# The second pair's second chunk takes its running sum from the whole first chunk instead of a carried row

## The chip, the cores and the metric

One core of a Trainium2 chip runs the whole program. The metric is the device time of one execution in microseconds (us). The core's engines are named as the profile names them: PE does matrix products, DVE is the vector engine, ACT the scalar engine, POOL the GpSimd engine, and SP only issues transfers. PEld is PE's weight load, which overlaps its products.

## What is computed

A linear attention with a complex decay feeds two layers of experts. Cut to what matters:

```python
mag = np.sqrt(a_re * a_re + a_im * a_im)
scale = np.minimum(mag, 0.999) / (mag + 1e-06)
a_re_n, a_im_n = (a_re * scale, a_im * scale)
for t in range(S):                       # S = 768, for 2 batches and 8 heads of 48
    S_re, S_im = (ar * S_re - ai * S_im + kv, ar * S_im + ai * S_re)
    y[:, :, t] = np.einsum('bhd,bhde->bhe', q[:, :, t], S_re)
h = x @ w_in                             # x: 1536 tokens x 384, w_in: 384 x 2048
x = (np.maximum(h, 0.0) + np.log1p(np.exp(-np.abs(h)))) @ w_out
for e in range(4):                       # four experts of 384 x 1024 x 384
    out += p[:, e:e + 1] * (np.maximum(x @ w1[e], 0.0) @ w2[e])
```

## The kernel before

**Attention in chunks.** The 1536 tokens are twelve chunks of 128, six to a batch. They are handled in six pairs `n` = 0 to 5, chunks `c` = 0 and 1 of each. The product of decays from the batch's start to a token is a running sum of logarithms: a phase (the angle, in `im`) and a magnitude (in `t`). `prefix(n, c, what)` makes the running sum inside a chunk by one product with a triangle of ones (`trik` for phases, `tri` for magnitudes) into a PSUM tile `pf` or `pl`. `wrap` takes whole turns out of the phase (ACT at L590, then DVE at L591), `level` copies the magnitude out (ACT, L597). `carry` takes the last row of both (ACT at L607 for the phase), and two small transfers on SP's queue (L608, L609) put them into the tile `rows`. The next chunk's `prefix` adds that row to its own first row with POOL (L564), so that the triangle product carries on from it.

Pair 0 does without a row: its second chunk's product starts with the whole first chunk times a matrix of ones (`onek` or `ones`, L582), and the triangle product adds to that. Pairs 3 to 5 split their operands in two (L570 on) and use a carried row too.

**Around it.** `squares`, `ratio` and `logmag` prepare angle and magnitude (POOL adds the two squares at L537 for every pair but the first). `trig` makes cosine and sine on ACT. Sine and arc tangent need another table of functions than exponential and logarithm, so both sit in an `excursion` between two table loads (L97). `s3_units` is the attention of one chunk: `prep` multiplies queries and keys by decay and angle (DVE, L643 and two of L655 into `QK`), `turn` transposes them on PE (L664, tile `tp`; ACT copies them out at L665), `score` makes the score products (`sp`, L673) that DVE masks into `A` (L674), `mix` makes the output `yps` (L689), `state` the running state `S` (`sps`, L700; DVE L704, L706), and `done` writes the output in two parts into `X`, the high one on ACT (L711), the low one on DVE (L712).

**Weights.** The first layer's weights come in as wide numbers. DVE joins them in three steps (L70, L71, L72 into `f`), ACT casts the high part (L181) and DVE subtracts for the low part (L182). Four pairs of such tiles (A and B) are needed for each block of the first layer, whose products are at L232 (into `h`) and L319 (into `y`). Every product of the first block, tokens 0 to 255, waits for `X` of pair 0.

**What sets the order.** The program is written as units, each put at a place on a time line (`put`), and the framework's scheduler then lays the instructions of each engine out in one order at build time. An engine runs its instructions strictly in that order. The three PSUM buffers of the tag `a` are handed out in turn to `pf`, `pl`, `sp`, `sps` and others. The change touches `prefix` and `s2_units`; the line that places the units of pair 1 stays, and spreads them from -8 to 0 on the time line:

```python
put([lambda: logmag(1, both)] + s2_units(1) + [lambda: s1_load(2), lambda: squares(2, both), lambda: ratio(2, both)]
    + [excursion(lambda: trig(1), lambda: arctan(2))], -8, 0)
```

## Time and profile before

| | |
|---|---|
| time, median of 3 runs | 737.78 us (737.22 to 738.26) |
| time of the profiled execution | 738.36 us |
| its span, first to last instruction | 736.6 us |
| PE busy | 702.5 us (95%) |
| DVE busy | 586.4 us (80%) |
| ACT busy | 487.4 us (66%) |
| POOL busy | 32.3 us (4%) |
| mean granted clock of PE | 0.988 |

The time is 1.8 us more than the span: that is what lies around the instructions. The span is read from the engine that is busy nearly all of it, PE, and a stretch is of interest where PE is not.

### The profile page before, as it was taken

How to read it: one execution, taken by the hardware profiler on the slowest of the kernel's cores; microseconds unless marked ns; L12 is line 12 of the kernel's file. 1: busy time of each engine (PE TensorE's matmuls, PEld its weight loads, DVE VectorE, ACT ScalarE, POOL GpSimd, SP SyncE). 2: the span in 40 equal slices, each digit the busy share in tenths (PEclk: the TensorE clock that was granted, in tenths of full speed). 3: DMA queues.
4: the chain of work that ended last, by engine and by line, in shares of the span. 5: the costliest groups of instructions: out<-in, count | busy, mean ns of one | idle time of the engine just before them, and what ended most of it. 6: DMA issues, size and time to landing. Idle time of an engine off the chain costs nothing.

```text
span 736.6 us, 13285 instructions
## 1 busy us (share of the span) xinstructions
PE 702.5 (95%) x5159; PEld 674.9 (92%) x5159; DVE 586.4 (80%) x1149; ACT 487.4 (66%) x898; POOL 32.3 (4%) x31
## 2 busy tenths in 40 slices
PE   2789999999999999999999999999999999999996
PEld 1468899999899999999999999999999999999996
DVE  6999999955875854548888779988778898998963
ACT  7887976888896856345686665555556567766640
POOL 1122010000111001000000000000000000000000
PEclk9699999999999999999999999999999999999998
DMA  7665666621211420121022120213445345455401
GB/s 268 195 191 179 201 203 192 224 77 44 86 45 59 122 80 2 59 86 44 23 86 65 43 87 21 87 44 109 119 157 155 127 151 172 150 172 152 162 31 69
DMA packets 36342, 83.56 MB, mean 113 GB/s; under 512 B 4528, under 2 KB 13232, under 8 KB 36272
## 3 DMA queue, kind: packets, MB, share of 16 engines
q1 hardware_dynamic: 36272, 82.64, 35.5%
q8 instruction: 42, 0.69, 0.4%
q14 instruction: 28, 0.23, 0.1%
HBM read 73.95 MB, written 8.65 MB: 112 GB/s over the span
## 4 chain that ended last, share of the span: by engine, by line


## 5 line engine op out<-in xcount | busy, mean ns | idle before, releaser
L232 PE MATMUL h<-X,A 128*128 128x384 f32 (+1 forms) x936 | 175.9, 329 | 2.3 <-ACT A L181 0.8
L232 PEld LDWEIGHTS h<-X,A 128*128 128x128 f32 x936 | 153.4, 188 | 5.6 <-issue 1.6
L319 PE MATMUL y<-B,g 128*128 128x384 f32 x744 | 150.2, 335 | 0.2 <-DVE acc L350 0.2
L319 PEld LDWEIGHTS y<-B,g 128*128 128x128 f32 x744 | 131.0, 188 | 0.7 <-issue 0.5
L319 PE MATMUL y<-g,B 128*128 128x384 f32 (+1 forms) x504 | 91.0, 315 | 0.3 <-ACT g L285 0.3
L319 PE MATMUL z<-B,g 128*128 128x384 f32 x372 | 84.7, 334 | 0.0
L319 PEld LDWEIGHTS y<-g,B 128*128 128x128 f32 x504 | 79.3, 189 | 2.0 <-ACT g L285 0.6
L319 PEld LDWEIGHTS z<-B,g 128*128 128x128 f32 x372 | 66.3, 188 | 0.0
L247 ACT ACTIVATE e<-h 128x384 f32<-128x384 f32 (+1 forms) x60 | 30.8, 512 | 37.1 <-PE h L232 36.0
L250 DVE SCALAR_TENSOR_TENSOR e<-h,e 128x384 f32<-128x384 f32 (+1 forms) x60 | 34.9, 581 | 20.6 <-ACT e L103 19.8
L255 DVE SCALAR_TENSOR_TENSOR g<-h,g 128x384 fp32r<-128x384 f32 x32 | 17.7, 555 | 28.1 <-ACT g L254 28.1
L103 ACT ACTIVATE e<-e,b_one 128x384 f32<-128x384 f32 (+1 forms) x60 | 38.2, 637 | 1.3
L103 ACT ACTIVATE e<-e 128x384 f32<-128x384 f32 (+1 forms) x60 | 32.8, 547 | 1.3
L415 PE MATMUL px<-X,sA 128*128 128x384 f32 x144 | 33.4, 340 | 0.0
L319 PE MATMUL z<-g,B 128*128 128x384 f32 x144 | 32.9, 335 | 0.0
L415 PE MATMUL px<-XC,sA 128*128 128x384 f32 x144 | 32.8, 336 | 0.0
L664 PE MATMUL tp<-ident,QK 128*96 128x128 f32 x192 | 27.2, 288 | 5.7 <-DVE QK L655 4.6
L664 PEld LDWEIGHTS tp<-ident,QK 128*96 128x96 f32 x192 | 22.2, 133 | 10.3 <-DVE QK L655 6.2
L254 ACT ACTIVATE g<-h 128x384 fp32r<-128x384 f32 x32 | 15.6, 488 | 21.3 <-PE h L232 21.1
L286 DVE TENSOR_TENSOR g<-e,g 128x384 fp32r<-128x384 f32 x48 | 26.6, 555 | 3.7 <-ACT g L285 2.9
L480 ACT CAST B<-rawB 128x768 fp32r<-128x768 f32 x24 | 20.0, 834 | 14.4 <-DMA rawB<-in_w_dram 7.3
L350 DVE SCALAR_TENSOR_TENSOR acc<-y,pr,acc 128x384 f32<-128x384 f32 x46 | 26.3, 612 | 1.7 <-PE y L319 1.7
(204 smaller groups left out, 1416.7 us busy)
## 6 DMA issues: line engine op xcount, KB each, us to landing
rawA<-in_w_dram SPq DMA_DIRECT2D x32, 384.0 KB, 3.0
rawB<-in_w_dram SPq DMA_DIRECT2D x32, 384.0 KB, 3.1
rawA<-in_w_in_dram SPq DMA_DIRECT2D x16, 384.0 KB, 3.5
rawB<-in_w_out_dram SPq DMA_DIRECT2D x16, 384.0 KB, 3.8
chkw<-in_w_in_dram SPq DMA_DIRECT2D x16, 384.0 KB, 3.2
chkw<-in_w_out_dram SPq DMA_DIRECT2D x16, 384.0 KB, 3.2
qk<-in_qkv_dram SPq DMA_DIRECT2D x12, 384.0 KB, 3.4
v<-in_qkv_dram SPq DMA_DIRECT2D x12, 256.0 KB, 2.9
```

The costliest lines, as they stand in the source:

```text
L103: i = nc.scalar.activation(out_, in_, fn, **kw)
L232: nc.tensor.matmul(ps, wt[:, p, kk, o:o + P], XB[b][:, q, kk, tok], start=(n == 0), stop=(n == 3 * KT - 1))
L247: nc.scalar.activation(t, h, AF.Abs)
L250: nc.vector.scalar_tensor_tensor(t, h, 0.0, t, ALU.max, ALU.add)
L254: nc.scalar.activation(g[:, 0, :], h, AF.Relu)
L255: nc.vector.scalar_tensor_tensor(g[:, 1, :], h, 0.0, g[:, 0, :].bitcast(F32), ALU.max, ALU.subtract)
L286: nc.vector.tensor_tensor(g[:, 1, :], t, g[:, 0, :].bitcast(F32), ALU.subtract)
L319: mm = nc.tensor.matmul(ys[j], l_, r_, start=(opens and n == 0 and not mate), stop=(closes and n == 2), skip_group_check=k == 0)
L350: nc.vector.scalar_tensor_tensor(dst, ys[j], pcol, dst, ALU.mult, ALU.add)
L415: nc.tensor.matmul(ps, lt[:, p, li, :], rhs, start=(start and n == 0), stop=(stop and n == 2), skip_group_check=True)
L480: nc.scalar.copy(hi, src)
L664: nc.tensor.transpose(tp[:96, hh, :], src[:, hf * 4 + hh, :], ident)
```

## The change

In pair 1, the second chunk no longer adds a carried row; its sum starts with the whole first chunk times a matrix of ones, as in pair 0. Since the first chunk holds the row carried from pair 0 in its first row, that is the same sum. The units of pair 1 are five instead of six: both phases' products, both `wrap`s, both magnitudes' products, both `level`s, and the carry to pair 2. The carry between the two chunks is gone.

```diff
         src = st[n][1 if what == 0 else 3]
-        if cc > 0 and n != 0:
+        if cc > 0 and n != 0 and (n, c) != (1, 1):
             row = src[0:1, c, :]
             nc.gpsimd.tensor_tensor(row, rows[0][0:1, what, :], row, ALU.add)
...
-        prev = range(c) if n == 0 else ()
+        prev = range(c) if n < 2 else ()
         for i in prev:
             nc.tensor.matmul(ps[:, :HD], lo, src[:, i, :], start=(i == 0), stop=False)
...
     def s2_units(n):
+        if n == 1:
+            return [lambda: (prefix(1, 0, 0), prefix(1, 1, 0)), lambda: (wrap(1, 0), wrap(1, 1)),
+                    lambda: (prefix(1, 0, 1), prefix(1, 1, 1)), lambda: (level(1, 0), level(1, 1)),
+                    lambda: carry(1, 1)]
         units = []
```

The scheduler lays out the first part of the program anew, on every engine. In the changed kernel, lines from `s2_units` on carry a number higher by four. Buffer numbers at the end of a name differ between the two. Two engines and three places matter below.

PE, from the first phase product of pair 1 to the scores of pair 0's first chunk, before (`tp_0_1` are transposes of pair 0's first chunk, `sp_0_0` and `sp_0_1` its scores):

```order
L583 MATMUL pf_0_243<-im_130,trik 128x384
L664 MATMUL tp_0_1_249<-ident,QK_0_221 96x128 x4
L664 MATMUL tp_0_1_256<-ident,QK_0_221 96x128 x4
L664 MATMUL tp_1_0_338<-ident,QK_1_325 96x128 x4
L664 MATMUL tp_1_0_345<-ident,QK_1_325 96x128
L583 MATMUL pl_0_246<-t_132,tri 128x384
L673 MATMUL sp_0_0_263<-qT_0_0_228,kT_0_0_235 128x128 x4
```

The same place after:

```order
L583 MATMUL pf_0_257<-im_130,trik 128x384
L582 MATMUL pf_1_259<-im_130,onek 128x384
L668 MATMUL tp_0_1_243<-ident,QK_0_221 96x128 x4
L583 MATMUL pf_1_259<-im_130,trik 128x384
L668 MATMUL tp_0_1_250<-ident,QK_0_221 96x128 x4
L677 MATMUL sp_0_0_263<-qT_0_0_228,kT_0_0_235 128x128 x4
L668 MATMUL tp_1_0_340<-ident,QK_1_326 96x128 x2
```

The two products of the second chunk's phase now stand between the transposes, and the magnitude product `pl_0` is gone from here; it stands with the second chunk's two behind pair 0's first state.

DVE, at the same time, before (`B_0` and `fA_1` belong to weights):

```order
L591 SCALAR_TENSOR_TENSOR im_130<-im_130,pf_0_243 128x384
L182 TENSOR_TENSOR B_0_473<-fB_0_0_478,B_0_473 128x384
L70 TENSOR_SCALAR fA_1_0_506<-rawA_1_0_502 128x384
L182 TENSOR_TENSOR B_0_473<-fB_0_1_491,B_0_473 128x384
L71 SCALAR_TENSOR_TENSOR fA_1_0_506<-rawA_1_0_502,fA_1_0_506 128x384
L674 TENSOR_TENSOR A_0_0_262<-sp_0_0_263,tri 128x512
L674 TENSOR_TENSOR A_0_1_269<-sp_0_1_270,tri 128x512
```

After:

```order
L591 SCALAR_TENSOR_TENSOR im_130<-im_130,pf_0_257 128x384
L678 TENSOR_TENSOR A_0_0_262<-sp_0_0_263,tri 128x512
L591 SCALAR_TENSOR_TENSOR im_130<-im_130,pf_1_259 128x384
L678 TENSOR_TENSOR A_0_1_269<-sp_0_1_270,tri 128x512
L182 TENSOR_TENSOR B_0_468<-fB_0_0_473,B_0_468 128x384
L182 TENSOR_TENSOR B_0_468<-fB_0_1_486,B_0_468 128x384
L70 TENSOR_SCALAR fA_1_0_501<-rawA_1_0_497 128x384
```

The four weight steps that stood ahead of the two masks now stand behind them, and the second chunk's L591 has come forward between the masks.

DVE again, up to the low part of `X` of pair 0's second chunk, on which the first layer's products wait, and the first step of pair 1's attention (`qk`), before:

```order
L71 SCALAR_TENSOR_TENSOR fB_1_0_558<-rawB_1_0_540,fB_1_0_558 128x384
L706 TENSOR_TENSOR S_321<-sps_1_440,S_321 96x512
L712 TENSOR_TENSOR X_119<-yps_1_397,X_119 128x3x128
L72 SCALAR_TENSOR_TENSOR fB_1_0_558<-rawB_1_0_540,fB_1_0_558 128x384
L71 SCALAR_TENSOR_TENSOR fB_1_1_579<-rawB_1_1_542,fB_1_1_579 128x384
L72 SCALAR_TENSOR_TENSOR fB_1_1_579<-rawB_1_1_542,fB_1_1_579 128x384
L643 SCALAR_TENSOR_TENSOR qk_0_224<-dec_0_532,qk_0_224 128x768
```

After:

```order
L71 SCALAR_TENSOR_TENSOR fB_1_0_553<-rawB_1_0_535,fB_1_0_553 128x384
L71 SCALAR_TENSOR_TENSOR fB_1_1_574<-rawB_1_1_537,fB_1_1_574 128x384
L72 SCALAR_TENSOR_TENSOR fB_1_0_553<-rawB_1_0_535,fB_1_0_553 128x384
L72 SCALAR_TENSOR_TENSOR fB_1_1_574<-rawB_1_1_537,fB_1_1_574 128x384
L710 TENSOR_TENSOR S_322<-sps_1_435,S_322 96x512
L716 TENSOR_TENSOR X_119<-yps_1_395,X_119 128x3x128
L647 SCALAR_TENSOR_TENSOR qk_0_224<-dec_0_527,qk_0_224 128x768
```

Three weight steps that stood between `X` and `qk` now stand ahead of `X`. On ACT, the cast of `X`'s high part has likewise moved behind the arc tangent of pair 2 and the table load that ends that excursion; before it stood ahead of both.

## Rows read from the trace of the kernel before

**Rows 1.** The page, part 1: busy time and share of the span.
```profile
PE 702.5 (95%) x5159; PEld 674.9 (92%) x5159; DVE 586.4 (80%) x1149; ACT 487.4 (66%) x898; POOL 32.3 (4%) x31
```
**Rows 2.** Stretches: length, PE, PEld, DVE, ACT, POOL busy, PE clock, DMA, GB/s.
```profile
50.00:60.00 10.00, 8.77 (x96) 8.30 (x100) 9.97 (x16) 9.94 (x19) 2.26 (x2) 1.00 0.58 176
60.00:70.00 10.00, 8.81 (x135) 7.28 (x124) 10.00 (x18) 5.36 (x11) 3.62 (x2) 1.00 0.51 159
70.00:80.00 10.00, 9.51 (x149) 7.78 (x149) 9.49 (x19) 8.90 (x17) 1.05 (x1) 1.00 0.71 247
80.00:100.00 20.00, 19.90 (x223) 18.51 (x216) 19.27 (x37) 18.63 (x35) 0.00 (x0) 1.00 0.64 201
```
**Rows 3.** PE's waits, 28 to 80 us: total, times, longest.
```profile
PE tp L664 <- DVE QK L655: 1.2, 1, 1.2
...
PE h L232 <- ACT A L181: 0.8, 1, 0.8
...
PE h L232 <- DVE A L182: 0.4, 1, 0.4
```
**Rows 4.** PE in order of time: start, length, what, idle before and releaser.
```profile
21.68 1.31 PE L583 MATMUL pf<-im,trik 128*128 128x384 f32 x2
26.41 1.94 PE L664 MATMUL tp<-ident,QK 128*96 128x128 f32 x8 [3.42 <-DVE QK L655]
29.13 1.65 PE L583 MATMUL pf<-im,trik 128*128 128x384 f32 x2 [0.78 <-POOL im L564]
...
49.99 4.09 PE L232 MATMUL h<-X,A 128*128 128x256 f32 x32 [0.26 <-DVE X L712]
55.31 1.96 PE L664 MATMUL tp<-ident,QK 128*96 128x128 f32 x16 [1.23 <-DVE QK L655]
```
**Rows 5.** DVE in order of time.
```profile
32.76 0.55 DVE L591 SCALAR_TENSOR_TENSOR im<-im,pf 128x384 f32<-128x384 f32 x1
...
37.16 1.14 DVE L72 SCALAR_TENSOR_TENSOR fA<-rawA,fA 128x384 int32<-128x384 int32 x1
38.23 1.16 DVE L70 TENSOR_SCALAR fA<-rawA 128x384 int32<-128x384 int32 x1
39.42 1.24 DVE L71 SCALAR_TENSOR_TENSOR fA<-rawA,fA 128x384 int32<-128x384 int32 x1
...
47.78 0.62 DVE L70 TENSOR_SCALAR fB<-rawB 128x384 int32<-128x384 int32 x2
48.33 0.54 DVE L71 SCALAR_TENSOR_TENSOR fB<-rawB,fB 128x384 int32<-128x384 int32 x1
48.80 0.68 DVE L706 TENSOR_TENSOR S<-sps,S 96x512 f32<-96x512 f32 x1
49.40 0.54 DVE L712 TENSOR_TENSOR X<-yps,X 128x384 fp32r<-128x384 f32 x1
...
52.10 0.95 DVE L643 SCALAR_TENSOR_TENSOR qk<-dec,qk 128x768 f32<-128x768 f32 x1
```
**Rows 6.** POOL in order of time.
```profile
36.07 1.82 POOL L537 TENSOR_TENSOR t<-t,t 128x768 f32<-128x768 f32 x1 [2.30 <-ACT t L536]
37.85 1.31 POOL L564 TENSOR_TENSOR im<-rows,im 1x384 f32<-1x384 f32 x1
39.13 1.10 POOL L564 TENSOR_TENSOR t<-rows,t 1x384 f32<-1x384 f32 x1
50.75 1.01 POOL L564 TENSOR_TENSOR im<-rows,im 1x384 f32<-1x384 f32 x1 [10.51 <-DMA v<-in_qkv_dram]
```
**Rows 7.** ACT in order of time, around the cast of X.
```profile
48.49 0.46 ACT L711 CAST X<-yps 128x384 fp32r<-128x384 f32 x1
48.84 0.85 ACT L103 ACTIVATE im<-im 128x768 f32<-128x768 f32 x1
49.71 1.28 ACT L97 ACT_TABLE_LOAD   x1
```
**Rows 8.** One stretch of 2 us, columns as in group 2.
```profile
26.00:28.00 2.00, 1.59 (x8) 1.46 (x8) 1.91 (x5) 1.92 (x5) 0.12 (x1) 0.53 0.15 22
```

## The prediction

> **What bounds the kernel.** I read the busy shares first: PE is busy for 702.5 of 736.6 us [rows 1], and 34 us are all that a change of order can win. Then the stretches: from 80 us on PE is busy for 19.90 of 20 us, while the three stretches of 10 us ahead of it lack 1.23, 1.19 and 0.49 us [rows 2]. So the change, which lies at about 28 to 50 us and shuffles the order for a while behind that, can win or lose only what PE waits before 80 us; work that reaches PE late there moves the whole rest. In those stretches DVE is busy for 9.97, 10.00 and 9.49 us of 10 [rows 2]: DVE, not PE, paces this part. The waits say the same: the transposes of pair 1 stand 1.2 us for `QK` from DVE, and first-layer products 0.8 and 0.4 us for the high and low parts of a weight, whose joining DVE does [rows 3]. Last I read DVE, POOL and ACT in order of time, to see what DVE does and what it loses.
>
> The sum is made against the profiled execution, 738.36 us (span 736.6 and 1.8 around it). The median of the runs is 0.58 lower, and I carry the difference over to it. What one can tell from no change is about 0.2%, 1.5 us.
>
> **Step 1, the added products.** Two products of ones are added, one per sum. A product of this shape takes 1.31 us in the row at 21.68 [rows 4], at the low clock; at the high clock I take half, 0.65 (an estimate). PE does not lack time here, but the first of the two stands between `pf_0` (started at 29.13 [rows 4]) and the transposes behind it, at the low clock. ACT's copy of these transposes stands ahead of its `wrap`, so `wrap` comes 1.2 to 1.3 us later, and DVE's L591, which started at 32.76 [rows 5], starts at about 34.0. In the new order nothing else of DVE's stands ahead of it, so DVE idles 1.2 us. Behind it come mask, L591, mask: two steps of 0.47 (start to start from 48.33 to 48.80 [rows 5]) and two of 0.60 (48.80 to 49.40, same width), 2.1 us. The scores come some 0.7 us late, since the second chunk's triangle product also stands ahead of them. I put the end of both masks at 36.9; before, DVE was through with them at 37.16 [rows 5]. The masks gain 0.3, because four weight steps moved behind them.
>
> **Step 2, what POOL takes from DVE.** POOL adds two squares at 36.07 for 1.82 us and then the two carried rows, 1.31 and 1.10 us at 37.85 and 39.13 [rows 6]. The three DVE steps of that time, L72, L70 and L71, take 1.14, 1.16 and 1.24 [rows 5]; the same steps elsewhere take 0.54 (L71, and I take the same for L72) and 0.31 or a little more (L70, two in 0.62). Each of them ends shortly behind POOL's: L72 at 38.30 where POOL ends at 37.89, L70 at 39.39 (39.16), L71 at 40.66 (40.23). DVE stood still till POOL was through. So they lost 0.60, 0.85 and 0.70, together 2.15 us. The two row additions go away: 1.55 us of DVE back. But the squares stay and move: DVE had spent most of their time on the masks, which read PSUM and were not held. Now DVE reaches its weight steps at 36.9, and POOL starts on the squares at about the same time (their ACT step stands behind the later `wrap`s): they cost their whole length, 1.8 us. Further, the row addition of pair 2 at 50.75 [rows 6], which follows the arc tangent, comes at about 48 and takes perhaps 0.4 us ahead of `X`. Ahead of `X`'s low part DVE thus loses 2.2 us instead of 2.15: what the change gives back there is taken again.
>
> [...]
>
> **Step 3, the first products of the first layer.** Before, 19 DVE steps lay from 37.16 to the low part of `X` at 49.40, 12.24 us without a gap [rows 5]. In the new order the four weight steps that moved behind the masks come in (two L182, L70, L71), and three more that stood behind `X` (L71, two L72); L591 has left. Six steps of 0.47 and one of 0.28 (L70, from 47.78 to 48.33 for two), less 0.47, make 2.6. From 36.9, 12.24 + 2.6 + 0.1 (step 2) lead to 51.8. `X`'s low part is there at 52.3 and the long run of L232 starts at 52.4 instead of 49.99 [rows 4]. The high part, on ACT at 48.49, has moved behind an arc tangent of 0.85 and a table load of 1.28 [rows 7]: at most 50.6, so it does not decide; nor does the decay behind it, which kept its place behind the table load.
>
> Right behind `X` DVE now goes on to `qk`, 0.47 later, at 52.3; before, it was there at 52.10 [rows 5], three weight steps later. So `QK` is 0.2 late, and pair 1's transposes could start at 55.5 instead of 55.31 [rows 4]. Ahead of them PE now has 26 of the 32 products of the run, 0.128 us each (4.09 for 32), 3.3 us: it gets there at 55.7, and the wait of 1.2 [rows 3] is gone. PE is 0.4 late, and the six products left over, 0.8, are still to be done: it lags by 1.2 us.
>
> **Step 4, what the waits behind it absorb.** From 60 to 80 us PE idles 1.68 us [rows 2], so there is room for the lag, but DVE has none: it is 0.2 late, its weight steps are as many as before, and the remaining additions on POOL catch it somewhere. At worst nothing sinks in, 1.2. At best all of it does, and the two waits for weights [rows 3], whose L70 to L72 now stand further ahead, go as well: 1.2 less 1.7, a gain of 0.5. I take the middle, **0.6 us slower**, since the lag is a delay of PE against a DVE that is nearly in time. Behind 80 us I add nothing: the work is the same, and PE hides it.
>
> Free are: the removed L607, its two transfers on SP and their successors moving up (in rows 3 PE waits for no transfer), the magnitude products and `level` of pair 1 (wanted only by the decay, behind the same table load), and the second product of ones, for which PE idles 1.2 us between 50 and 60 us alone. If PE had no such cover, the second would cost its 0.65.
>
> The sum: 738.36 + 0.6 = 739.0 for a profiled execution, **738.4 us** for the median.
>
> **The rivals.**
>
> *DVE's relief reaches PE (faster).* Here the squares on POOL fall on steps that read PSUM, as before (0.60 lost, not 1.8), so `X` is there at 51.1 and `QK` about 1.0 before my time, 0.8 ahead of the old one. Then PE lags only by the six products less some 0.7, that is nothing at the transposes, and all 1.68 us of waits from 60 to 80 us may go: 1.7 faster, 736.1. For it speaks that DVE paces this stretch and loses two holds; against it the order of DVE, in which seven of the eight steps behind the masks read SBUF only.
>
> [...]
>
> [...]
>
> *The lag stays and grows (slower).* A weight of the first layer or a mask at 60 to 80 us comes later than before, since DVE works on other weights first; each such wait costs what [rows 3] shows, 0.4 to 0.8, on top of 1.2: 1.8 slower, 739.6.
>
> *Nothing reaches the end.* All lag sinks in, no gain: 737.8.
>
> **Chances.** The forecast with its neighbours, from 0.5 faster to 1.4 slower (737.3 to 739.2), including the case of nothing: 0.52. DVE's relief: 0.20. The clock: 0.10. The growing lag: 0.18. The cases outside 1.5 us are the second, the third and the fourth: faster by over 0.2% 0.20, within 0.2% 0.52, slower 0.28. The range reaches from the relief's 736.1 to the clock's 740.1; two cases of ten lie beyond at its ends.
>
> **What would show it.** Two more products of L582, one right behind `pf` at about 30.4; two POOL additions less; the squares of pair 2 on POOL at about 36.9 with a weight step of DVE that ends just behind them; the long run of L232 at 52.4; the transposes of pair 1 at 55.7 with no wait before; 60 to 80 us with less than 1.7 us of idle PE. I am wrong in step 2 if the weight steps run beside the squares, in step 3 if `X`'s low part is there by 51, and in step 4 if PE's waits from 60 to 80 us grow.

## The result, and the profile after

The changed kernel takes 743.82 us (median of 8 runs, 740.77 to 746.62) where the kernel before takes 737.74 (8 runs on the same chip). The ratio is 1.0077, with a 95% interval of 1.0053 to 1.0100: 5.7 us slower. The forecast was 738.4, the top of the range 740.1. The profiled execution took 743.01 us, 741.3 of them in the span.

The page's first part, against [rows 1]:

```profile
PE 706.1 (95%) x5163; PEld 678.6 (92%) x5163; DVE 584.8 (79%) x1149; ACT 486.6 (66%) x897; POOL 34.9 (5%) x29
```

Four matrix instructions more (two products of two each), two POOL additions less, one ACT instruction less: the change was made as written. Yet POOL is busy for longer with fewer instructions. The stretches, columns as in [rows 2]; the first three of 1 us show the clock where it fell and came back:

```profile
44.00:45.00 1.00, 0.82 (x6) 0.53 (x6) 1.00 (x2) 1.00 (x4) 0.00 (x0) 1.00 1.02 254
46.00:47.00 1.00, 1.00 (x6) 1.00 (x6) 0.96 (x2) 0.80 (x2) 0.00 (x0) 0.50 0.50 183
52.00:53.00 1.00, 1.00 (x51) 1.00 (x45) 1.00 (x3) 0.00 (x0) 0.00 (x0) 1.00 0.00 0
50.00:60.00 10.00, 9.41 (x150) 8.65 (x148) 9.34 (x17) 7.65 (x15) 0.56 (x1) 0.90 0.49 142
60.00:70.00 10.00, 10.00 (x158) 8.27 (x158) 10.00 (x19) 7.01 (x14) 4.29 (x2) 1.00 0.52 175
70.00:80.00 10.00, 8.24 (x63) 7.29 (x62) 9.63 (x18) 5.74 (x12) 4.70 (x2) 1.00 0.74 251
80.00:100.00 20.00, 17.93 (x238) 17.36 (x238) 19.19 (x37) 19.85 (x35) 0.00 (x0) 1.00 0.59 183
200.00:300.00 100.00, 99.93 (x917) 94.93 (x917) 65.04 (x102) 72.82 (x120) 11.15 (x9) 1.00 0.20 63
```

The clock's column is not whole in this trace. It shows 1.00 throughout 28 to 38 us, yet the phase products at 29.32 and 30.76 below last 1.65 and 1.49 us, as the same shape does at 18.96 and 20.40 us in before, where the column shows 0.50. So the low clock is read here from the lengths of products too, and the mean clocks of two traces are not compared.

From 60 to 80 us PE idles 1.76 us, hardly more than the 1.68 of [rows 2]. From 80 to 100 it idles 2.07, where it idled 0.10. From 200 to 300 us PE is busy for 99.93 of 100: nothing is given back there. PE in order of time, with its waits, against [rows 4]:

```profile
29.32 1.65 PE L583 MATMUL pf<-im,trik 128*128 128x384 f32 x2 [0.78 <-POOL im L564]
30.76 1.49 PE L582 MATMUL pf<-im,onek 128*128 128x384 f32 x2
...
34.97 1.06 PE L677 MATMUL sp<-qT,kT 96*128 96x128 f32 x8
...
44.17 0.64 PE L668 MATMUL tp<-ident,QK 128*96 128x128 f32 x4 [2.17 <-ACT qT L669]
...
45.96 1.91 PE L677 MATMUL sp<-qT,kT 96*128 96x128 f32 x8
...
48.39 2.08 PE L677 MATMUL sp<-qT,kT 96*128 96x128 f32 x8
...
55.01 3.38 PE L232 MATMUL h<-X,A 128*128 128x256 f32 x26 [0.59 <-DVE X L716]
58.23 1.47 PE L668 MATMUL tp<-ident,QK 128*96 128x128 f32 x12
...
76.88 0.91 PE L583 MATMUL pf<-im,trik 128*128 128x384 f32 x2 [1.21 <-POOL im L564]
...
93.16 0.98 PE L232 MATMUL h<-X,A 128*128 128x256 f32 x6 [2.07 <-DVE e L250]
```

ACT at the first of these waits, against [rows 7]:

```profile
42.25 1.28 ACT L97 ACT_TABLE_LOAD   x1
43.54 0.58 ACT L669 COPY qT<-tp 96x512 f32<-96x512 f32 x1
...
53.15 0.48 ACT L715 CAST X<-yps 128x384 fp32r<-128x384 f32 x1 [2.35 <-PE yps L693]
```

DVE and then POOL, against [rows 5] and [rows 6]:

```profile
34.23 0.56 DVE L591 SCALAR_TENSOR_TENSOR im<-im,pf 128x384 f32<-128x384 f32 x1 [1.34 <-ACT im L590]
36.06 0.69 DVE L678 TENSOR_TENSOR A<-sp,tri 128x512 f32<-128x512 f32 x1 [1.27 <-PE sp L677]
36.67 0.54 DVE L591 SCALAR_TENSOR_TENSOR im<-im,pf 128x384 f32<-128x384 f32 x1
37.17 0.69 DVE L678 TENSOR_TENSOR A<-sp,tri 128x512 f32<-128x512 f32 x1
37.78 2.64 DVE L182 TENSOR_TENSOR B<-fB,B 128x384 fp32r<-128x384 f32 x2
...
47.91 0.69 DVE L678 TENSOR_TENSOR A<-sp,tri 128x512 f32<-128x512 f32 x1 [0.33 <-PE sp L677]
...
50.50 0.69 DVE L678 TENSOR_TENSOR A<-sp,tri 128x512 f32<-128x512 f32 x1 [1.44 <-PE sp L677]
...
54.41 0.54 DVE L716 TENSOR_TENSOR X<-yps,X 128x384 fp32r<-128x384 f32 x1
```

```profile
37.86 2.14 POOL L537 TENSOR_TENSOR t<-t,t 128x768 f32<-128x768 f32 x1 [3.90 <-ACT t L536]
...
72.13 3.30 POOL L564 TENSOR_TENSOR t<-rows,t 1x384 f32<-1x384 f32 x1 [7.04 <-DMA rows<-t]
75.40 1.43 POOL L564 TENSOR_TENSOR im<-rows,im 1x384 f32<-1x384 f32 x1
```

**Reading it in order of time.** The first product of ones and the triangle product behind it stand among the transposes and delay the first `wrap` and the scores: DVE idles 1.34 us ahead of the one and 1.27 ahead of the other. At 42.25 ACT loads a function table for 1.28 us. The copies of the transposes `qT` stand behind that load in ACT's order, so PE waits 2.17 us. Then PE's granted clock is at 0.50 from about 45 to 52 us: score products that took 1.06 at 34.97 take 1.91 and 2.08. DVE waits 0.33 and 1.44 for those scores, and `X` is 5.0 us late. The delay at the places that both kernels have:

| start of | before | after | later |
|---|---|---|---|
| DVE L591, pair 1 | 32.76 | 34.23 | 1.5 |
| DVE `X` low, pair 0 | 49.40 | 54.41 | 5.0 |
| PE long run of L232 | 49.99 | 55.01 | 5.0 |
| DVE second step of `QK`, pair 1, first chunk | 54.30 | 57.08 | 2.8 |
| the same, second chunk | 67.72 | 70.62 | 2.9 |
| DVE `e`, next two halves of the first layer | 77.24, 87.46 | 81.75, 92.43 | 4.5, 5.0 |
| ACT first copy of the first layer's `Y` | 95.22 | 100.39 | 5.2 |
| ACT cast of a later `X` | 221.07 | 225.88 | 4.8 |

So the delay is 5.0 at `X`, but only 2.8 on DVE behind it, since three weight steps had been done ahead of `X`. Behind 70 us it grows to 5 again, and stays there, 4.8 still at 226 us.

DVE's account explains most of this. Two stretches, columns as in [rows 2], run from its first step of `QK` of pair 0 (0.20 us later in the change) to the first copy of `Y`, before and after:

```profile
24.07:95.22 71.15, 62.49 (x762) 53.28 (x762) 68.95 (x121) 62.56 (x108) 13.28 (x10) 0.95 0.62 192
24.27:100.39 76.12, 66.42 (x770) 57.29 (x771) 70.16 (x124) 63.01 (x109) 14.29 (x8) 0.96 0.59 185
```

DVE idles 5.96 us there instead of 2.20, 3.76 more, and is busy 1.21 longer, with three steps more: together the 5.0. The idle time is added ahead of `X` (4.78 instead of 0.99); behind `X` DVE idles 1.18 instead of 1.21, so nothing there gives it back.

### The profile page after: what moved, and what is told of

Its sections match the earlier page's. It is cut to its first block, busy times and chain, and to the rows that moved or that the text cites. A ratio compares the mean times of both kernels' runs of the same rounds, so it can differ in the third digit from the quotient of the medians.

```text
span 741.3 us, 13288 instructions
## 1 busy us (share of the span) xinstructions
PE 706.1 (95%) x5163; PEld 678.6 (92%) x5163; DVE 584.8 (79%) x1149; ACT 486.6 (66%) x897; POOL 34.9 (5%) x29
## 4 chain that ended last, share of the span: by engine, by line
## 5 line engine op out<-in xcount | busy, mean ns | idle before, releaser
L232 PE MATMUL h<-X,A 128*128 128x384 f32 (+1 forms) x936 | 176.3, 329 | 2.7 <-DVE e L250 2.1
L232 PEld LDWEIGHTS h<-X,A 128*128 128x128 f32 x936 | 153.6, 189 | 6.7 <-DVE e L250 2.4
L668 PEld LDWEIGHTS tp<-ident,QK 128*96 128x96 f32 x192 | 22.5, 133 | 10.8 <-DVE QK L659 4.8
L480 ACT CAST A<-rawA 128x384 fp32r<-128x384 f32 (+1 forms) x48 | 20.1, 457 | 11.4 <-DMA rawA<-in_w_dram 9.1
```

The costliest lines, as they stand in the source:

```text
L232: nc.tensor.matmul(ps, wt[:, p, kk, o:o + P], XB[b][:, q, kk, tok], start=(n == 0), stop=(n == 3 * KT - 1))
L480: nc.scalar.copy(hi, src)
L668: nc.tensor.transpose(tp[:96, hh, :], src[:, hf * 4 + hh, :], ident)
```

## The experiments

Two theories were open. **A**: `X` is late, by the table load and the low clock, and that delay passes through whole. **B**: the delay at `X` is half made good, as [rows 4] suggested, and the loss is made behind 69 us, where the order is new as well. Later came **C**, that it is DVE's idle time ahead of 56 us, and **D**, that it is the low clock alone; **E** and **F** put B at one half of the first layer's products. The rival to all is that no single place decides.

### The scheduler left to lay the order

**e1_ones_old_units**: the product of ones with the old six units.

```diff
     def s2_units(n):
-        if n == 1:
-            return [lambda: (prefix(1, 0, 0), prefix(1, 1, 0)), lambda: (wrap(1, 0), wrap(1, 1)),
...
-            if (CH[n] + c) % CB < CB - 1:
+            if (CH[n] + c) % CB < CB - 1 and (n, c) != (1, 0):
```

> The second chunk of pair 1 takes its prefix by the matrix of ones, but its steps come in the old order (both prefixes of the first chunk, its wrap and magnitude, then the second chunk). Before 737.7 us, after 743.8. Theory A (the loss is the delay of X's low part of pair 0, made by where the first products and the weight steps fall, and it passes whole to the end): the products of ones go behind pair 0's first state here, X's low part comes by 51 us and the long run of up-projection products by 52, so 737 to 739.5. Theory B (the loss is made by waits at 70 to 95 us, for POOL's sum of squares and for VectorE's activations): X early or late changes nothing, and the time stays above 741 as long as those waits stand. If the matrix of ones itself costs the time, 743 too.

It took 8645.74 us and measures nothing: `wrap` of pair 1 writes over the phases in place, so the second chunk's product of ones summed wrapped phases, and the guard in the kernel sent it through its slow general path. It shows one thing: both phase products must stand ahead of the first `wrap`, so the new units belong to the matrix of ones and can't be undone alone.

**e2_order_carried**: the carried row kept, the order by phases.

```diff
-        if cc > 0 and n != 0 and (n, c) != (1, 1):
+        if cc > 0 and n != 0:
...
-        prev = range(c) if n < 2 else ()
+        prev = range(c) if n == 0 else ()
...
+    def carry_row(n, c, what):
...
-            return [lambda: (prefix(1, 0, 0), prefix(1, 1, 0)), lambda: (wrap(1, 0), wrap(1, 1)),
-                    lambda: (prefix(1, 0, 1), prefix(1, 1, 1)), lambda: (level(1, 0), level(1, 1)),
-                    lambda: carry(1, 1)]
+            return [lambda: prefix(1, 0, 0), lambda: wrap(1, 0), lambda: carry_row(1, 0, 0),
+                    lambda: prefix(1, 0, 1), lambda: level(1, 0), lambda: carry_row(1, 0, 1),
+                    lambda: prefix(1, 1, 0), lambda: wrap(1, 1),
+                    lambda: prefix(1, 1, 1), lambda: level(1, 1), lambda: carry(1, 1)]
```

> The other part alone: the carried row stays, with its two adds on POOL; of pair 1's first chunk the phase's prefix, wrap and row go ahead of the magnitude's, and then the second chunk follows likewise. Theory A: the place of the first score products and of X's low part decides; it stands behind pair 0's masks as before, so X's low part by 51.5 us and 737 to 740. If the order by phases is what costs: X's low part near 54 us and 742 to 745. Theory B: by the waits at 70 to 95 us, with no tie to X's low part.

740.13 against 739.23 us, ratio 1.0010 (1.0000 to 1.0019). Eleven units in a stretch laid out for six pushed pair 1's sines behind their first reader: DVE's `QK` of pair 1 starts at 51.28, ACT's step that makes its input at 52.26. The kernel leaves the sines out of `QK`, so this is no clean measure.

**e3_fill**: nine idle products behind the transposes that PE waited on.

```diff
+FILL = 9
...
-                    nc.tensor.transpose(tp[:96, hh, :], src[:, hf * 4 + hh, :], ident)
+                    last = nc.tensor.transpose(tp[:96, hh, :], src[:, hf * 4 + hh, :], ident)
...
+            if (n, c, hf) == (0, 1, 0):
+                fill = psum.tile([P, 2, 512], F32, tag="y", name="fill", bufs=1)
+                for _ in range(FILL):
+                    behind(nc.tensor.matmul(fill[:, 0, :P], tri, ones, start=True, stop=True), last)
```

> The changed kernel, with nine idle 128 x 128 products (a result that nothing reads) put on TensorE behind the first transposes of pair 0's second chunk, into the stretch of 2.17 us in which it waited for the copy of qT. Theory A with the clock as part of the delay: the granted clock stays at 1.00 from 44 to 52 us, the score products of that chunk take 1.1 us per eight in place of 1.9 to 2.1, X's low part comes some 2 us earlier (52 to 52.5 us) and the time falls by 1.5 to 3 us against the changed kernel, to 741 to 742.3. Theory B: the scores are faster, but the time stays within 0.7 us of 743.8. If the clock falls all the same, no idle time of TensorE was its cause.

742.16 us, ratio 1.0038 (1.0022 to 1.0054). The order was laid anew around the products; the clock then fell at 49.4 to 52.9 us, behind a wait of 1.36 for `kT`. It can't tell the clock from the order.

**e4_table_behind**: the table load behind the copies.

```diff
-                nc.scalar.copy(dst, tp[:96])
+                cp = nc.scalar.copy(dst, tp[:96])
+                if (n, c) == (0, 1):
+                    st.setdefault("copies", []).append(cp)
...
+            for i in st.pop("copies", ()):
+                behind(tabs["load"], i)
```

> The changed kernel, with ScalarE's second table load (1.28 us, ahead of the sines of pair 1) held behind the four copies of qT and kT of pair 0's second chunk. Theory A: TensorE's wait of 2.17 us for qT goes to under 1 us, the clock holds to 52 us, X's low part comes by 51.5 to 52.5 us, and the time falls by 2.5 to 5 us, to 739 to 741.5. Theory B: X's low part is earlier, but the time stays within 1 us of 743.8, or the sines of pair 1 come later and it grows.

741.1 us, ratio 1.0017 (1.0004 to 1.0029), 1.3 us slower than before: the best order seen for the changed kernel's own instructions. But its profiled execution (742.71) still has a wait of 1.99 us for `qT` at 44.20: the load has moved to 46.39, and in its place a cast (L181, 43.16) that waits 1.24 for DVE stands ahead of that copy. So the time falls in A's range, but the gain isn't the one meant, and that trace, slower than the median, doesn't show where it comes from.

### The order written down

To move one thing at a time, each engine's instructions were from here on chained in the order that the scheduler had laid, by a dependency meant to add no wait:

```python
for x, y in zip(row_, row_[1:]):
    tc.add_manual_dep(y, x.name, NOSYNC, ...)
```

The diffs below show rows of an engine's order. No run has the order written down and nothing moved, so that this costs nothing is not shown by a time; in g10's trace DVE's rows keep the spacing of before up to its edit at 69 us.

**g1_fill**: the idle products of e3 alone, the rest of the changed kernel as it stood.

```diff
 PE  tp (pair 0, second chunk, first half)
+PE  fill<-ones,tri x9
 PE  tp (second half)
```

> The changed kernel with its order of instructions written down for every engine, so that nothing else moves, and nine idle 128 x 128 products on TensorE in the 2.17 us in which it waited for the copy of qT (42.0 to 44.2 us). Theory A (X's low part of pair 0 is late because the order leaves TensorE waiting and the granted clock falls behind that, and the delay passes whole to the end): the clock stays at 1.00 to 52 us, both score groups take 1.1 us, X's low part comes at 52 to 52.8 in place of 54.41, and the time falls by 1.6 to 2.4 us, to a ratio of 1.0045 to 1.0055. Theory B (later waits at 70 to 95 us cost the time, X's delay is absorbed): X as under A, the ratio stays at 1.007 to 1.008.

1.0079 (1.0062 to 1.0096). The wait for `qT` was filled, the clock held from 44 to 52 us, and `X` came a microsecond earlier, at 53.36. Nothing was won, against A's 1.0045 to 1.0055: the clock fell at 93 to 97 us instead, behind a wait of 2.28 for `e`.

**g2_x_early**: the changed kernel with `X` ahead of six weight steps, and the table load behind the copies.

```diff
 DVE
+L710 S, L716 X
 L70 fB x2, L71 fB x2, L72 fB x2
-L710 S, L716 X
 ACT
-L97 table load
 L669 qT, kT, qT, kT
+L97 table load
```

> The changed kernel with its order written down, but ScalarE's second table load stands behind the four copies of qT and kT of pair 0's second chunk, and VectorE's six weight steps (L70 to L72 on fB) behind X's low part. Theory A: no wait of 2.17 us on TensorE, the clock holds, X's low part at 50 to 51 us (3.4 to 4.4 us earlier), and the time falls by as much, to a ratio of 1.0015 to 1.0035. Theory B: the ratio stays above 1.006.

1.0081 (1.0064 to 1.0098): no gain, though `X` came 3.0 us earlier, at 51.37. PE in order of time shows where that went:

```profile
51.97 3.37 PE L232 MATMUL h<-X,A 128*128 128x256 f32 x26 [0.43 <-DVE X L716]
...
57.55 2.39 PE L668 MATMUL tp<-ident,QK 128*96 128x128 f32 x12 [2.21 <-DVE QK L659]
```

PE now waits for `QK`, which stands behind the weight steps, and behind that wait the clock is at 0.50 from 58 to 61 us. Theory A fails on the changed kernel.

**g4_x_late**: the mirror of it on the kernel before.

```diff
 DVE
-L706 S, L712 X
 L72 fB, L71 fB, L72 fB
+L706 S, L712 X
```

> The kernel before with its order written down, but three weight steps of VectorE (L72, L71, L72 on fB, 2.35 us in the trace of before) stand ahead of the sum of states and X's low part of pair 0's second chunk instead of right behind them. Nothing is added, only X's low part comes later, at 51.6 to 51.8 us in place of 49.40. Theory A: the delay passes whole, a ratio of 1.0025 to 1.0035. The prediction's step 4 (half of it is absorbed at 60 to 80 us): 1.0005 to 1.0015. Theory B: 1.000 to 1.001.

1.0026 (1.0012 to 1.0041), 1.9 us slower, which is A's number, though the interval still holds the upper end of the half (1.0012 to 1.0015). `X` is 2.4 us late, counted from an early DVE step as in the table further down (52.77 by the trace's own zero). PE:

```profile
50.74 0.74 PE L232 MATMUL h<-X,A 128*128 128x256 f32 x4 [0.72 <-ACT X L711]
53.37 5.59 PE L232 MATMUL h<-X,A 128*128 128x256 f32 x32 [1.89 <-DVE X L712]
```

The 32 products take 5.59 instead of 4.09 [rows 4], the clock at 0.50 from 54 to 57 us. So the clock can fall right at the first layer's first products: here with `X` at 52.77 and behind a wait of 1.89, shorter than the 3.42 of [rows 4] behind which [rows 8] shows 0.53.

**g5_fill3**: idle products at the three places where the clock had fallen or threatened to.

```diff
 PE  tp (pair 0, second chunk, first half)
+PE  fill x9
...
 PE  h<-X,A x4 (the high part)
+PE  fill x7
 PE  h<-X,A x26
...
 PE  h (ahead of the wait for e at 91 us)
+PE  fill x8
```

> The changed kernel, order written down, with idle products in three of TensorE's long waits: nine at 42 us (as in the first filled run), seven in the wait for X's low part near 52 us, eight in the wait for VectorE's activation near 92 us (24 products more, with a result that nothing reads). Theory D (each wait of about 2 us lets the granted clock fall for 3 to 7 us, filling one only moves the fall to the next, and those falls are the loss): the clock stays at 1.00 from 34 to 130 us and the ratio comes down to 1.002 to 1.0045. Theory C (the loss is idle time of VectorE ahead of 56 us, 4.1 us more of it than before, which nothing behind gives back): no fall, but the ratio stays at 1.005 to 1.008.

742.83 us, 1.0067 (1.0048 to 1.0085). Its stretches, columns as in [rows 2]:

```profile
30.00:40.00 10.00, 10.00 (x115) 7.25 (x115) 7.44 (x13) 7.41 (x14) 3.06 (x2) 1.00 0.72 241
40.00:60.00 20.00, 19.33 (x235) 16.96 (x234) 19.97 (x37) 18.75 (x32) 2.21 (x3) 1.00 0.55 166
60.00:100.00 40.00, 37.90 (x493) 34.67 (x496) 39.20 (x70) 32.69 (x61) 5.41 (x4) 1.00 0.60 193
```

From 34 us on the clock does not fall (the score products at 45.63 and 46.97 last 1.06 and 1.16 us), and 4.9 of the 5.7 us remain. The idle products aren't in the way, as PE's waits show: behind each of the three PE still waits a little.

```profile
PE h L232 <- DVE X L724: 0.4, 1, 0.4
PE h L232 <- DVE e L250: 0.4, 1, 0.4
PE tp L668 <- ACT qT L669: 0.2, 1, 0.2
```

In the change's trace the low clock amounts to 3.4 us, half of the 7 at 0.50 from 45 to 52; taken away, it gave back about 1 (0.8 by the ratios, which their intervals don't tell from nothing, 1.2 by the profiled executions, 743.01 and 741.85). Theory D fails as the whole cause. The ratio is the one that C gave, but C fails too: DVE idles only 1.3 us more than before up to the first copy of `Y`, and that copy is still 3.4 late. What 24 idle products may cost by themselves was not measured.

**h1_before_order**: the changed kernel's instructions in the order of before; what is new stands where it can earliest.

```diff
 PE  pf (first chunk)
+PE  pf (second chunk: onek, trik)
...
-PE  pl (first chunk)
...
+PE  pl (first chunk), pl (second chunk: ones)
 PE  pl (second chunk: tri)
 DVE L591, L182, L70, L182, L71, L678, L678
+DVE L591 (second chunk)
```

> The changed kernel's instructions in the order that the kernel before had on every engine: the products of ones and of the second chunk's phase stand right behind the first chunk's phase prefix, the magnitudes' three products where the second chunk's stood, and the wraps and copies follow their products; all else stands as before. If the matrix of ones itself costs the time: TensorE's two products more at the low clock (2.9 us) push the scores, masks and X's low part by 2 us or more, ratio 1.003 or over. If the new order was the cause (theory A as to its place): the masks wait 1 to 1.5 us for the transposes, X's low part comes by 50.5 us, ratio 0.999 to 1.002.

741.4 us, 1.0037 (1.0023 to 1.0051): 2.7 slower than before, 3.0 less than the change's own order. DVE:

```profile
35.99 0.55 DVE L591 SCALAR_TENSOR_TENSOR im<-im,pf 128x384 f32<-128x384 f32 x1 [2.62 <-ACT im L590]
40.76 1.27 DVE L678 TENSOR_TENSOR A<-sp,tri 128x512 f32<-128x512 f32 x2
```

With weight steps again between L591 and the masks, DVE's idle time ahead of L591 is passed to the masks (40.76 instead of 36.06), and PE waits 2.91 us for them. `X` is 4.3 late and the ratio over 1.003, as expected if the products themselves cost the time at this place.

**h3_products_at_39** and **h2_products_late**: both phase products moved behind the masks, with a PSUM tile of their own; h3 in the order of before otherwise, at some 39 us, h2 in the order of the change.

```diff
 h3, PE
-pf (first chunk)
...
+pf (first chunk), pf (second chunk: onek)
 pf (second chunk: trik)
 h2, PE
-pf (first chunk), pf (second chunk: onek, trik)
 tp, sp (pair 0, first chunk)
+pf (first chunk), pf (second chunk: onek, trik)
 h2, ACT
-L590, L590, L181, L181
 L669 kT, qT, kT (pair 0, first chunk)
+L590, L590 (casts between the copies)
```

> The changed kernel's instructions in the order of the kernel before, but with all six prefix products of pair 1 at the places of the second chunk's two (39 to 42 us in the kernel before), the first chunk's wrap and copy just ahead of the second's, and the phases in the two idle banks of y. So nothing of pair 1 stands ahead of pair 0's transposes and scores. If the place of the products of ones was the cause of the loss ahead of 57 us: VectorE's idle time from 32 to 38 us under 1 us, X's low part by 50.5 us, ratio 0.998 to 1.002. If the matrix of ones costs by itself, wherever it stands: X's low part at 52 us or later and ratio 1.003 or over.

> The changed kernel, order written down, but the three phase products of pair 1 (first chunk, ones, second chunk) stand behind the scores of pair 0's first chunk instead of among its transposes, and their wraps behind VectorE's first two masks; the products get the two idle banks of y, so that no buffer holds the scores up. Theory C: VectorE's idle time between 32 and 38 us falls from 2.6 to under 1 us, both masks of the first chunk come 1.5 to 2.5 us earlier, and the ratio comes down from 1.0077 to 1.003 to 1.0055. Theory D: the wait for the copy of qT behind the table load stays, the clock falls there as before, and the ratio stays at 1.006 to 1.008.

h3 took 741.52 us, 1.0048 (1.0035 to 1.0061), and h2 748.7, 1.0146 (1.0123 to 1.0169), the slowest of all. In h2 ACT's `wrap`s, which now wait for the late products, stand ahead of the copies that PE waits for:

```profile
47.68 1.09 PE L673 MATMUL tp<-ident,QK 128*96 128x128 f32 x4 [4.16 <-ACT qT L674]
```

In h3 the six products stand ahead of the scores of pair 0's second chunk, which start at 45.42 instead of 42.18 in before, and DVE waits for them:

```profile
46.51 0.69 DVE L683 TENSOR_TENSOR A<-sp,tri 128x512 f32<-128x512 f32 x1 [2.43 <-PE sp L682]
```

h3's numbers are those expected if the products cost by themselves wherever they stand (`X` at 52.95, over 1.003). Against that stands e4: the same products at 1.0017 (1.0004 to 1.0029), clear of h3's interval. The later place was no cheaper in either order: h1's 2.7 against h3's 3.5, which their intervals don't tell apart, and the change's 5.7 against h2's 10.8.

**k1_after_warm** and **k2_before_warm**: idle products at 13 to 25 us in both kernels, to see what the products of ones cost at the high clock.

```diff
+PE  fill x22 (at some 13 us)
 PE  pf (pair 0)
+PE  fill x12 (at some 22 us)
 PE  tp (pair 0)
```

> The changed kernel, order written down, with 22 idle products ahead of the first phase product (a wait of 5.96 us) and 12 ahead of the first transposes (3.22 us), so that TensorE comes to the products of ones at the full clock. If the low clock at 26 to 33 us is what makes the products of ones dear (1.49 us each against 0.81 at the full clock): the transposes' last group ends 1.5 to 2.5 us earlier, the masks with it, VectorE's idle time at 32 to 38 us falls under 1 us, ratio 1.003 to 1.0055. If their number or place is: 1.007 to 1.008.

> The kernel before, order written down, with the same 22 and 12 idle products. VectorE idles only 0.5 us between 26 and 60 us there, so a faster TensorE at 19 to 33 us finds it busy: ratio 0.998 to 1.0005. If TensorE's clock in that stretch bounds the kernel before: its masks come 1 us or more earlier and the ratio is 0.9965 to 0.998.

k1 took 1.0095 (1.0076 to 1.0114), k2 742.28 us, 1.0052 (1.0032 to 1.0072); both miss. Pair 0's phase products (the one at 21.68 in [rows 4]) then took 0.81 instead of 1.31, but pair 1's was slow again, as k2's PE shows:

```profile
21.72 2.84 PE L769 MATMUL fill<-ones,tri 128*128 128x128 f32 x24
27.11 1.29 PE L664 MATMUL tp<-ident,QK 128*96 128x128 f32 x8 [2.56 <-DVE QK L655]
29.83 1.65 PE L583 MATMUL pf<-im,trik 128*128 128x384 f32 x2 [1.43 <-POOL im L564]
```

The row of pair 1 is 1.65 as without them, so what was asked is not shown. Instead, with 34 idle products the kernel before was 3.8 us slower while `X` came in time (0.05 late). Of the 2.6 us of its profiled execution 0.7 lie ahead of 25 us already, and 1.2 arise at 77 us, where PE waited 1.31 for a POOL addition that it did not wait for in before. k2 moves nothing there, so why this one was late, and the rest, stays open.

### Behind 69 us

In the changed kernel seven of nine products of one half of the first layer (`h`) stand behind pair 2's phase product at 76.88, which waits for POOL; ACT's steps on that half and DVE's `e` follow.

**g10_half_late**: that alone, on the kernel before.

```diff
 PE
-h x9
 pf (pair 2, second chunk)
+h x7
 pl (pair 2, second chunk)
+h x2
 ACT
-L247, L103, L103, L97 table load
 L590, L597
+L247, L103, L103, L97 table load
 DVE
-L250 e
 L591
+L250 e
```

> The mirror image, on the kernel before with its order written down: the same nine products go behind the second chunk's phase prefix of pair 2 (two of them behind the magnitude's), and ScalarE's and VectorE's steps on them behind that prefix's wrap and copy, the table load behind those, as they stand in the changed kernel. Everything ahead of 69 us stands as before. Theory E: the activation at 77.24 us comes at 80 to 81, the one at 87.46 at 89 to 91, ratio 1.0015 to 1.0035. Theory A: ratio 0.999 to 1.001.

742.02 us, 1.0062 (1.0047 to 1.0077), 4.6 slower, though all is as before up to 69 us, `X` included. PE:

```profile
83.56 0.86 PE L232 MATMUL h<-X,A 128*128 128x256 f32 x5 [1.24 <-DVE A L182]
85.82 0.38 PE L232 MATMUL h<-X,A 128*128 128x256 f32 x1 [1.40 <-ACT A L181]
```

So a loss can be made here alone, by weights that come late; this is what B asks for, though the ratio is above E's 1.0015 to 1.0035. Its size is less sure: the profiled execution was the fastest of six (739.98 to 745.43), 1.6 slower than that of before. There the first copy of `Y` came at 99.42 instead of 95.22, a delay of 4.2 (3.6 from the early DVE step), and a later cast of `X` at 117.93 instead of 115.00, 2.9: a part is given back behind 100 us.

**g9_half_first**: the reverse on the changed kernel.

```diff
 PE
+h x9
 pf (pair 2, second chunk)
-h x7
 pl (pair 2, second chunk)
-h x2
```

(ACT's three steps and DVE's `e` move ahead of L590 and L591 likewise.)

> The changed kernel, order written down, with one thing moved: the nine up-projection products of the third half tile (h of 77.33 and 78.82 us) stand ahead of the second chunk's phase prefix of pair 2, which waited 1.21 us for POOL's row add, and what ScalarE and VectorE do to their result (L247, two of L103, L250) stands ahead of that prefix's wrap. Theory E (the second half of the loss is made there: TensorE, ScalarE and VectorE queue that half tile behind a prefix that waits for POOL): the activation of VectorE comes 2 to 3 us earlier than 81.75, the next one 2 us earlier than 92.43, TensorE's wait of 2.07 us at 91 to 93 goes under 0.5, and the ratio falls from 1.0077 to 1.004 to 1.006. Theory A (all of it is made ahead of 57 us): ratio 1.007 to 1.0085.

743.21 us, 1.0062 (1.0048 to 1.0077): by the ratios 1.1 of the 5.7 us comes back, which the intervals don't tell from nothing, so the time decides little. DVE:

```profile
79.39 0.67 DVE L250 SCALAR_TENSOR_TENSOR e<-h,e 128x512 f32<-128x512 f32 x1
...
92.91 0.69 DVE L250 SCALAR_TENSOR_TENSOR e<-h,e 128x512 f32<-128x512 f32 x1
```

The first `e` came 2.4 us earlier, as expected, but the next one, 92.43 in the change, did not. The six weight steps and the `wrap` that stood ahead of the first `e` now stand between the two, DVE idles only 0.46 us there, and ACT waits 1.69 us for a weight step ahead of its table load. So the gain is handed back, and B fails as the one cause.

**g11_half_first_fill** adds g1's nine idle products to g9, **g12_wrap_first** moves ACT's excursion forward as well, **g13_wrap_first_table** has g12 and the table load of 42 us behind the copies.

```diff
 g11: g9, and
+PE  fill x9 (as in g1)
 g12: g9, and on DVE L591 behind e, the next e ahead by five steps, on ACT
 L597
+L97 table load, L275 g, |im|
 L181 A, L181 A
-L97 table load
 L715 X
-L275 g, |im|
 g13: g12, and
-L97 table load (at 42 us)
 L669 qT, kT, qT, kT
+L97 table load
```

> The first kernel of this call (the half tile ahead of the prefix) and the nine idle products at 42 us of the first filled run together. Theory E with the clock: the fill alone gave nothing, since the fall moved to the wait at 91 us; with that wait gone too it should stay away, X's low part comes 1 to 1.5 us earlier, and the ratio falls below that of the first kernel, to 1.002 to 1.0045. If X's low part does not matter: the same ratio as the first kernel.

> The kernel with the half tile ahead of the prefix, and further, behind 74 us only: VectorE's second wrap of pair 2 stands ahead of the six weight steps (L70 to L72 on fA) that it followed, its activation of the half tile after (92.43 us) ahead of three more weight steps and L647; ScalarE's table load and the Abs of the sines stand ahead of the two casts that wait for those weight steps. Theory F (the half tile alone gave only 1 us since ScalarE's table load and pair 2's sines, queued behind casts that wait for VectorE's weight steps, still held the next half tile back): ScalarE's idle time of 1.7 us there goes, the activation of 92.43 comes at 89 to 90.5, TensorE's wait of 2.0 us goes under 0.7, the first copies of Y come by 98.5 us in place of 100.39, ratio 1.002 to 1.0045. If only what lies ahead of 57 us counts: 1.006 to 1.008.

> The same, and ScalarE's second table load behind the four copies of qT and kT of pair 0's second chunk (42 us), which the earlier run with X's low part early had together with VectorE's weight steps moved; those stay here, so that VectorE has work while it waits for the states. TensorE's wait of 2.17 us goes under 0.9, VectorE's idle time of 1.44 us at 49 to 50.5 goes, the QK products of pair 1 come 1.2 to 2 us earlier than 56.21. If the front part (theory A) and the back part (theory F) add: ratio 0.9995 to 1.0025. If the front part gives nothing: that of the first kernel of this call.

They took 1.0086 (1.0068 to 1.0104), 1.0116 (1.0095 to 1.0137) and 1.0095 (1.0078 to 1.0113). Another wait came beside the one aimed at; the two longest of PE in g12 behind 70 us are

```profile
PE y L319 <- ACT g L275: 2.5, 1, 2.5
PE h L232 <- DVE e L250: 1.7, 1, 1.7
```

the first of them new. These three miss, and the order behind 69 us was not mended by them.

**All together.** `X` and the first copy of `Y` are the delay against the kernel before, each counted from the same early DVE step of its own execution, the first of `QK` (24.07 in before); the profiled time is that less 738.36; the loss is the ratio less one, times 737.7. "DVE idle" is its idle time from that step to the first copy of `Y`, less the 2.20 of before. All in us.

| kernel | `X` low | first `Y` | DVE idle | profiled | loss |
|---|---|---|---|---|---|
| the change | 4.8 | 5.0 | 3.8 | 4.7 | 5.7 |
| g1, one fill | 3.3 | 5.5 | 3.3 | 7.5 | 5.8 |
| g2, X early | 1.2 | 5.0 | 4.0 | 4.5 | 6.0 |
| g5, clock held | 3.3 | 3.4 | 1.3 | 3.5 | 4.9 |
| h2, products late | 8.7 | 9.9 | 8.1 | 10.1 | 10.8 |
| k1, warm | 3.7 | 4.8 | 3.0 | 4.4 | 7.0 |
| g9, half first | 3.7 | 6.7 | 4.5 | 6.3 | 4.6 |
| g11, half first and fill | 2.8 | 4.3 | 2.1 | 3.9 | 6.3 |
| g12, wrap first | 2.3 | 8.7 | 6.2 | 10.1 | 8.6 |
| g13, wrap first and table | 2.7 | 7.6 | 5.2 | 7.1 | 7.0 |
| g4, X late (on before) | 2.4 | 3.5 | 3.8 | 2.5 | 1.9 |
| g10, half late (on before) | 0.0 | 3.6 | 3.3 | 1.6 | 4.6 |
| k2, warm (on before) | 0.1 | 1.4 | 1.2 | 2.6 | 3.8 |
| h1, order of before | 4.3 | 4.4 | 4.8 | 3.9 | 2.7 |
| h3, products at 39 | 3.0 | 4.2 | 4.4 | 2.6 | 3.5 |
| e3, fill, own order | 2.9 | 2.0 | 2.8 | 4.8 | 2.8 |
| e4, table behind, own order | 3.8 | 4.9 | 4.7 | 4.4 | 1.3 |

`X`'s delay does not order the losses. The first copy of `Y` goes with the profiled time within 1.1 us in all but g1, g10, g12, h3, k2 and e3. A profiled execution can stand some microseconds from the median (g10, e3 and e4 most), so a single trace shows where time went better than how much.

What the first `Y` does follow is DVE. In the five kernels with the order of before (g4, g10, k2, h1, h3) it is late by what DVE idles more, within 0.4 us, wherever that idle time lies. In the ten with the order of the change it is 1.0 to 2.5 us later than that, and there DVE has done three more steps ahead of it. So g2 won nothing by an earlier `X`: DVE idled 4.0 us more instead of 3.8, 1.2 of it now behind `X`. Each idle time has a wait of its own behind it, so this says which engine carries the loss, not which wait is to blame.

## Why the prediction was wrong

**The bound** was read rightly in kind: DVE paces the first part, and PE took what was lost there through to the end. But the line was drawn at 80 us ("only what PE waits before 80 us"), and the 2.07 us of PE's idle time that before does not have lie behind it, at 91 to 93.

**Step 1** held. L591 started at 34.23 (34.0 forecast) and DVE idled for it. The triangle product's 1.65 and the product of ones' 1.49 are the low clock's size, as at 18.96 and 20.40 us in before, where the column shows 0.50. For the high clock the estimate of 0.65 fits the spacing of two such products in k2, 0.64 from 20.43 to 21.07. But the masks, put at an end of 36.9, ended at 37.8: for the late scores the sum had "some 0.7", and DVE idled 1.27 ahead of the first mask.

**Step 2** held in kind. POOL's squares came at 37.86 (36.9) and lasted 2.14 us. The two L182 beside them took 2.64 us, where two of them take 1.02 at 82.36, and ended 0.4 behind POOL. Two masks took 1.44 us at 35.81 in before, in part beside POOL's squares at 36.07, and 1.27 at 77.64 in the change with POOL idle, so "not held" is nearly what the rows show. The traces show which steps last longer beside each other, not by what. So against the 2.15 us that DVE had lost beside POOL's steps ahead of `X`, it lost 1.6 again; the forecast was 2.2.

**Step 3** was mis-sized: "lead to 51.8" for `X`'s low part, which started at 54.41, so 5.0 late instead of 2.4. The DVE steps (19 and 7 more, less one) were counted rightly, and 0.9 of the miss came from step 1. Most of the rest is that the sum gave DVE no gap. It now had gaps of 0.33, 1.44 and 0.16 for PE's products, because PE had first waited 2.17 us for a copy behind ACT's table load and then worked at a granted clock of 0.50. The prediction read ACT's order only at the cast of `X`, not at the transposes' copies. The transposes of pair 1 did find no wait (58.23), as step 3 had it.

**The clock** was given 0.10 and the upper end of the range, 740.1. No run shows the 1.7 us by which that stands above the forecast. What the runs show is that the clock falls in the change, to 0.50 from about 45 to 52 us behind the wait of 2.17, and in g4 from 54 to 57, where 32 products took 5.59 us instead of 4.09, 1.5 more. g5 then shows that the clock is not the cause of most of the loss: its column stands at 1.00 from 34 us on, and 4.9 of the 5.7 us remain.

**The rival of the growing lag**, given 0.18, came nearest: slower, since DVE works on other weights first. It was priced at 1.8 us, by the two waits for weights of [rows 3]; the first layer's products waited 2.07 us in one, for `e`, and the lag on DVE grew from 2.9 at 71 us to 5.0 at 92.

**Step 4** failed. It held that half of a lag of 1.2 us sinks in ("the middle", though the middle of its own 1.2 and -0.5 is 0.35), and that "behind 80 us I add nothing: the work is the same, and PE hides it". Neither came: the lag, 5.0 at `X`, is 5.2 at `Y` and 4.7 at the end. Its own test, PE's waits from 60 to 80 us growing, did not speak: 1.76 against 1.68. The loss showed behind it, where PE's 2.07 for `e` at 93.16 has no counterpart in before. The work is the same there, but its order is not: g10 shows that part of this order alone, in a kernel that is in time up to 69 us, can cost 4.6 us by the ratio (1.6 by its profiled execution). And the lag found nothing to sink into, since DVE, which carries it, idles 1.2 us between `X` and the first `Y` in either kernel; PE's idle time, from which step 4 took its half, is not the room that counts. Up to 100 us three engines hand work to each other in strict order, and in no run did a lag sink in whole: where a delay was taken out at one place (g2, g9, g1), a wait for the next engine took its place.

**What the matrix of ones itself costs**, less what the carried row gives back, is at most e4's 1.3 us (0.3 to 2.1 by its interval), since e4 has all of the change's instructions; this takes for granted that e4's order wins nothing that the kernel before could have won as well, which no run shows. On that footing 4.4 of the 5.7 us belong to the order that the scheduler laid around them, or 3.6 with e4 at the end of its interval; the 5.7 are themselves known to 3.9 to 7.4 only. By order alone (in h2 with PSUM banks of their own for two products) the changed kernel's instructions lost from 1.3 (e4) to 10.8 us (h2), and those of the kernel before 1.9 (g4) and 4.6 (g10). That no single place decides is what the runs leave standing; what the places share is DVE. Which part of the new order costs how much stays open: the shares measured one by one (h1's 3.0, g10's 4.6, and g9's and g5's 1, neither clear of noise) don't add up, and a part that is undone alone brings back less than it costs when it is done alone. No version beat the kernel before.

## What to carry to other kernels

When a change makes a scheduler lay the program anew, the work that it adds can be the smaller part of its price, as it seems to be here: read, for every engine that feeds another, what now stands ahead of each copy and each mask, and look above all for long steps that can't be moved aside (a table load ahead of copies, here 1.28 us, a `wrap` that waits for a late product). A lag that a prediction lets sink into idle time needs slack on every engine of the chain, not on the last one; here DVE was busy for 10.00 of 10 us beside PE's gaps (60 to 70 us, [rows 2]), and its idle time, added up to a place that both kernels have, told the delay there better than any single row. To tell the price of the work from that of the order, write the order down and move one thing at a time, on both kernels: the mirror on the kernel before told more here (g4, g10) than the repair on the changed one.

## What was not expected of the hardware

The clock fell behind single waits shorter than the 3.42 us of [rows 4]: 1.36 (e3, at 0.50 from some 49.4 to 52.9 us), 1.89 (g4, 54 to 57), 2.17 (the change, 45 to 52) and 2.28 us (g1, 93 to 97). Behind 2.07 us at 93 in the change, and behind 1.23 at 55 us in before [rows 4], the column stayed at 1.00 (the next six products took 0.98 us in the change, 1.34 in g1): in these runs the length of the wait alone doesn't tell. In k2 idle products ended 2.56 us ahead of the next work; the phase product at 29.83, behind one more wait of 1.43, took 1.65 us all the same.

POOL's steps vary in length as DVE's do: the addition of one row took 0.98 us at 49.58, while DVE waited, and 3.30 at 72.13 beside DVE's weight steps; in all POOL was busy for 34.9 us instead of 32.3 with two instructions less. Of DVE, two L182 took 1.81 us at 75.91, beside POOL's addition at 75.40, where two take 1.02 at 82.36 with POOL idle.
